# First FFT stage in bursts of eight tile matmuls, and the filters in four parts

## The chip, the cores and the metric

The kernel runs on one core of a Trainium2 chip. The metric is the time of one execution in microseconds; lower is better. The profile's span, from the first to the last instruction, is 1.7 to 1.9 us shorter than this time.

## The reference

A frequency filter over the sequence, then a dense layer with exact GELU and a second dense layer:

```python
X = np.fft.rfft(x, axis=1)                      # x: 8 images of 3008 x 256
y = np.fft.irfft(X * (filt_r + 1j * filt_i)[None], n=3008, axis=1)
h = y.reshape(24064, 256) @ w_in                # w_in: 256 x 2048
g = 0.5 * h * (1 + erf(h / sqrt(2)))
out = g @ w_out                                 # w_out: 2048 x 256, float32 out
```

## The kernel before

The transform of 3008 = 47 x 64 is done by matmuls in four stages with a reload through DRAM after the first and after the third. Image 0 is transformed in a head of its own. Images 1 to 7 are transformed under the dense layers: each step ("slot") of these emits four matmuls of the second layer (`mm2`, L493) and one product of the first (`mm1`, L466), and a table of slots says where the pieces of the transform go in between. In the traces TensorE's matmuls follow one another in the order in which they are emitted.

The first stage works with 47 x 48 tables, so the array is used as four tiles of 64 x 64 (the "tile mode"), each of which takes one matmul. The four start within 10 ns of one another in the trace; such a group is called a burst here:

```python
def s1(self, b, u):
    ...
    ps = [self.bank("ps_s1") for h in range(2)]          # two of three shared banks
    c, i = u // 2, 2 * (u % 2)
    for r in range(2):
        for h in range(2):
            w = 8 * c + 4 * r + i
            nc.tensor.matmul(ps[h][64 * r:64 * r + 64, :], lhsT=self.T1s[64 * h:64 * h + NA],
                             rhs=x[64 * h:64 * h + NA, w:w + 2, :], start=True, stop=True)
    for h in range(2):
        self._evac(a[:, h, i:i + 2, :].rearrange("p a b -> p (a b)"), ps[h], False)   # VectorE
    ...  # after every second burst: four stores of a to DRAM (R1)
```

The matmuls write to PSUM, in eight banks, and VectorE's copies out of it (`_evac`, "casts" in the views) make a bank free again. The banks belong to the first dense layer (three), the second (two) and the shared pool `f` (three). In the head they belong to other pools, `v` (five) and `t` (three):

```python
m.psum(wide, v=(5, 1), t=(3, 1))
for u in range(10):
    if u < 8:
        m.c3t(u)
    if u >= 2:
        m.c4(u - 2, (act, False if u > 7 else act))
wide.close()
m.psum(ctx, h=(3, 1), o=(2, 1), f=(3, 1))
```

The slots (`hi` is the first slot of the tokens of image b; `r1` and `r2` are the reloads, `s2` and `s4` the second and fourth stage):

```python
if b == 1:
    s1, n1, r1, s2, n2, r2, s4, n4 = 0, 1, 16, 26, 2.8, 61, 68, 0.72
else:
    s1, n1, r1, s2, n2, r2, s4, n4 = hi - 94, 1, hi - 78, hi - 71, 3.5, hi - 26, hi - 17, 1
```

## Time and profile before

| | before |
|---|---|
| median of the timed runs | 780.6 us |
| span of the profiled run | 780.6 us (this run took 782.4 us) |
| TensorE matmul busy | 98% |
| bursts of the first stage, images 1 to 7 | 56, of four matmuls |
| first weight load of the first dense layer | at 40.8 us |

TensorE is busy from 41 us to the end, so what counts is how long its stream is and where it waits. Three things are read in the prediction: what a burst adds to a slot, the wait ahead of the second stage (L300), and VectorE's filter products in the head.

### The profile page before, as it was taken

Reading aid. Unit: us, or ns where it says so; the run is one execution under the profiler, and the core shown is the slowest. Engines: PE = TensorE matmul, PEld = TensorE weight load, DVE = VectorE, ACT = ScalarE, POOL = GpSimd, SP = SyncE. Lnnn points to the kernel's source line nnn. Section 1 sums busy time; section 2 is a strip of 40 time slices with the busy share of each in tenths; the row PEclk is TensorE's granted clock in tenths of the full one; section 3 lists DMA queues with packets and bytes.
Section 4 is the critical chain, followed back from the end, with each engine's and each line's share of the span. In section 5 each row is a group of like instructions: output and inputs, shape, how many; then the busy total and the mean of one; then the engine's idle time right before and its main releaser. Section 6 shows DMA issues by size and latency. Waiting matters only on the chain.

```text
span 780.6 us, 14960 instructions
## 1 busy us (share of the span) xinstructions
PE 764.2 (98%) x5965; PEld 528.7 (68%) x6066; DVE 400.7 (51%) x722; ACT 568.4 (73%) x980; POOL 63.1 (8%) x157
## 2 busy tenths in 40 slices
PE   8999999999999999999999999999999999999998
PEld 5847665676766766577676767667776676766666
DVE  7866755473555635466354663546635465410011
ACT  6879855897558975589656896569865798666663
POOL 7801100020000100011000110001100000000000
PEclk9999999999999999999999999999999999999999
DMA  9794744465145651546515464255542522401111
GB/s 145 136 198 113 148 123 109 134 138 142 46 113 151 126 151 34 149 121 129 136 48 163 104 118 135 65 166 101 115 126 78 149 81 69 122 30 39 41 42 55
DMA packets 87270, 85.66 MB, mean 110 GB/s; under 512 B 6688, under 2 KB 77472, under 8 KB 87200
## 3 DMA queue, kind: packets, MB, share of 16 engines
q1 hardware_dynamic: 78816, 68.70, 31.0%
q0 software_dynamic: 8384, 16.00, 14.1%
q8 instruction: 47, 0.77, 0.4%
q14 instruction: 23, 0.19, 0.1%
HBM read 54.00 MB, written 46.66 MB: 129 GB/s over the span
## 4 chain that ended last, share of the span: by engine, by line
PE 86%; DMA 7%; POOL 2%; issue 1%; ACT 1%; DVE 1%; SPq 1%; POOLq 0%
PE ps_o L493 40%; PE ps_h L466 36%; PE ps_s L350 3%; DMA b_sb<-R 3%; PE ps_s L277 2%; PE ps_s L300 2%; PE ps_s L325 2%; DMA x_sb<-in_x_dram 2%; DMA R<-a_sb 1%; DMA F<-in_filt_i_dram 1%; POOL x_sb L82 1%; POOL F L96 1%; ACT g_sb L469 1%; SPq L286 1%; DVE a_sb L251 0%
## 5 line engine op out<-in xcount | busy, mean ns | idle before, releaser
L469 ACT ACTIVATE g_sb<-ps_h 128x512 bf16<-128x512 f32 x752 | 438.9, 597 | 189.4 <-PE ps_h L466 162.8
L493 PE MATMUL ps_o<-w_out_sb,g_sb 128*128 128x256 bf16 x2992 | 447.8, 273 | 3.6
L466 PE MATMUL ps_h<-y_sb,w_in_sb 128*128 128x512 bf16 (+3 forms) x1500 | 424.9, 365 | 0.4 <-DVE y_sb L253 0.4
L493 PEld LDWEIGHTS <-g_sb 128*128 128x128 bf16 x2992 | 282.1, 98 | 132.0 <-issue 10.9
L466 PEld LDWEIGHTS <-w_in_sb 128*128 128x128 bf16 x1600 | 154.5, 98 | 23.3 <-issue 1.6
L499 DVE COPY ost<-ps_o 128x512 f32<-128x512 f32 x93 | 63.8, 686 | 142.6 <-PE ps_o L493 141.1
L308 DVE TENSOR_TENSOR p<-ps_s,F 128x512 bf16<-128x512 f32 x84 | 58.0, 691 | 98.1 <-ACT p L307 85.1
L253 DVE TENSOR_SCALAR y_sb<-ps_s 128x376 bf16<-128x376 f32 x112 | 60.9, 548 | 80.8 <-PE ps_s L350 80.8
L251 DVE CAST a_sb<-ps_s 128x512 bf16<-128x512 f32 x112 | 72.1, 686 | 39.6 <-PE ps_s L277 38.4
L251 DVE CAST v_sb<-ps_s 128x512 bf16<-128x512 f32 x84 | 56.9, 684 | 4.5 <-PE ps_s L325 4.5
L306 ACT ACTIVATE p<-ps_s 64x512 bf16<-64x512 f32 x84 | 49.9, 594 | 2.9 <-PE ps_s L300 0.7
L307 ACT CAST p<-ps_s 64x512 bf16<-64x512 f32 x84 | 48.5, 577 | 1.0
L350 PEld LDWEIGHTS <-d_sb 96*128 96x128 bf16 x448 | 30.8, 97 | 25.6 <-DMA d_sb<-R 0.6
L101 POOL COPY gate<-p 1x1 bf16<-1x1 bf16 x48 | 8.5, 177 | 475.4 <-DVE p L310 475.4
L350 PE MATMUL ps_s<-T,d_sb 96*128 96x94 bf16 x448 | 36.3, 204 | 1.2
L310 DVE TENSOR_TENSOR p<-p 128x512 bf16<-128x512 bf16 x84 | 35.7, 425 | 2.9
L309 DVE TENSOR_TENSOR p<-p,F 128x512 bf16<-128x512 bf16 x84 | 34.8, 415 | 0.0
L300 PE MATMUL ps_s<-b_sb,T 128*128 128x256 bf16 x168 | 32.1, 272 | 1.9 <-DMA b_sb<-R 1.8
L82 POOL DMA_DIRECT2D x_sb<-in_x_dram x64 | 32.6, 511 | 13.3 <-issue 12.2
L325 PE MATMUL ps_s<-p,T 128*128 128x256 bf16 x168 | 32.1, 273 | 0.1
L325 PEld LDWEIGHTS <-T 128*128 128x128 bf16 x168 | 16.4, 98 | 20.1 <-DVE p L310 0.5
L300 PEld LDWEIGHTS <-T 128*128 128x128 bf16 x168 | 16.4, 98 | 16.2 <-issue 3.5
(103 smaller groups left out, 194.2 us busy)
## 6 DMA issues: line engine op xcount, KB each, us to landing
out_dram<-ost SPq DMA_DIRECT2D x93, 256.0 KB, 2.5
x_sb<-in_x_dram POOLq DMA_DIRECT2D x64, 188.0 KB, 3.9
R<-a_sb SPq DMA_DIRECT2D x112, 96.0 KB, 2.1
b_sb<-R SPq DMA_DIRECT2D x28, 384.0 KB, 4.5
R<-v_sb SPq DMA_DIRECT2D x42, 256.0 KB, 3.4
d_sb<-R SPq DMA_DIRECT2D x56, 192.0 KB, 4.8
w_in_sb<-in_moe_w_in_dram POOLq DMA_DIRECT2D x2, 512.0 KB, 10.4
w_out_sb<-in_moe_w_out_dram POOLq DMA_DIRECT2D x2, 512.0 KB, 11.1
```

What stands on the lines that cost most here:

```text
L251: self.nc.vector.tensor_copy(out=out, in_=in_)
L253: self.nc.vector.tensor_scalar(out=out, in0=in_, scalar1=scale, scalar2=None, op0=ALU.mult)
L300: nc.tensor.matmul(ps[:, 256 * i:256 * i + 256], lhsT=self.T2[:, k, 1:3].rearrange("p a b -> p (a b)"), rhs=self.st[b, "b", k // 6][:, k % ...
L306: nc.scalar.activation(out=p2[0:64], in_=ps[64:128], func=AF.Copy, scale=-1.0)
L307: nc.scalar.copy(out=p2[64:128], in_=ps[0:64])
L308: nc.vector.tensor_tensor(out=p1, in0=ps, in1=f(0), op=ALU.mult)
L325: nc.tensor.matmul(ps[:, 256 * i:256 * i + 256], lhsT=self.T3[:, k].rearrange("p a b -> p (a b)"), rhs=w[:, 256 * i:256 * i + 256], start= ...
L350: nc.tensor.matmul(ps[:, 94 * i:94 * i + 94], lhsT=d[:, (grp % 2) * 4 + i, 128 * half:128 * half + 128], rhs=t4, start=True, stop=True)
L466: nc.tensor.matmul(ps[:, o:o + n], lhsT=self.w_in_sb[:, dc, jc * 128:jc * 128 + 128], rhs=self.ring[:, dc, off:off + n], start=(dc == 0), ...
L469: nc.scalar.activation(out=self.st["g", t][:, jc, :], in_=ps, func=AF.Gelu)
L493: nc.tensor.matmul(ps[:, tile_i % 2, :], lhsT=g[:, jc, tile_i * 128:tile_i * 128 + 128], rhs=self.w_out_sb[:, jc, :], start=(jc == 0), sto ...
L499: nc.vector.tensor_copy(out=ost, in_=ps)
```

## The change

The intent: enter and leave the tile mode half as often, by doing two bursts in one. That takes four banks, one of which the dense layers lend. Around it the slots move, and in the head the filters come in smaller parts, with the copies arranged so that the filter products wait less.

```diff
-        ps = [self.bank("ps_s1") for h in range(2)]
-        c, i = u // 2, 2 * (u % 2)
... (signature, a's tile and the old loops left out)
+        ps = [[self.bank("ps_s1", "h" if i == h == 0 else "f") for h in range(2)] for i in range(2)]
+        for i in range(2):
+            for r in range(2):
+                for h in range(2):
+                    w = 8 * c + 4 * r + 2 * i
+                    nc.tensor.matmul(ps[i][h][64 * r:64 * r + 64, :], ...)
+        for i in range(2):
+            for h in range(2):
+                self._evac(a[:, h, 2 * i:2 * i + 2, :]..., ps[i][h], False)
... (stores as before, now after every burst)
-    for k, n in ((0, 4), (4, 8), (12, 12)):
+    for k, n in ((0, 4), (4, 4), (8, 8), (16, 8)):
         m.load_filters(k, n)
+    m.dup_filters(nc.gpsimd, 4, 4)
     m.load_w_in()
-    m.dup_filters(nc.gpsimd, 4, 8)
+    m.dup_filters(nc.gpsimd, 8, 8)
... (in the loop: dup_filters(16, 8) ahead of T1p, T1q and T1s in place of
     dup_filters(12, 4) ahead and dup_filters(16, 8) after; table_4 at q == 6, not q == 3)
-            s1, n1, r1, s2, n2, r2, s4, n4 = 0, 1, 16, 26, 2.8, 61, 68, 0.72
+            s1, n1, r1, s2, n2, r2, s4, n4 = 0, 4, 15, 25, 2.8, 61, 68, 0.72
-            s1, n1, r1, s2, n2, r2, s4, n4 = hi - 94, 1, hi - 78, hi - 71, 3.5, hi - 26, hi - 17, 1
+            s1, n1, r1, s2, n2, r2, s4, n4 = hi - 94, 3.5, hi - 80, hi - 69, 3.5, hi - 24, hi - 17, 1
```

More of the change, by code (lines that the diff above doesn't have):

```diff
@@ L262, in table_1_tiles, with s1 @@
             v.tensor_copy(out=self.T1s[r:r + NA, 0:48], in_=self.T1[0:NA, 0:48])
-    def s1(self, b, u):
+    def s1(self, b, c):
         nc = self.nc
-        if u % 2 == 0:
-            self.st[b, "a"] = self.pa.tile([128, 2, 4, 256], BF16, tag="a", name="a_sb")
-        if u == 0:
+        if c == 0:
             self.st[b, "R1"] = self.dram.tile([NB, 48, 256], BF16, tag="R1", name="R1")
-        a, R1, x = self.st[b, "a"], self.st[b, "R1"], self.st[b, "x"]
-        ps = [self.bank("ps_s1") for h in range(2)]
-        c, i = u // 2, 2 * (u % 2)
+        a = self.pa.tile([128, 2, 4, 256], BF16, tag="a", name="a_sb")
+        x = self.st[b, "x"]
+        ps = [[self.bank("ps_s1", "h" if i == h == 0 else "f") for h in range(2)] for i in range(2)]
[3 more added lines that the diff above has]
+                    w = 8 * c + 4 * r + 2 * i
+                    nc.tensor.matmul(ps[i][h][64 * r:64 * r + 64, :], lhsT=self.T1s[64 * h:64 * h + NA],
+                                     rhs=x[64 * h:64 * h + NA, w:w + 2, :], start=True, stop=True)
+        for i in range(2):
+            for h in range(2):
+                self._evac(a[:, h, 2 * i:2 * i + 2, :].rearrange("p a b -> p (a b)"), ps[i][h], False)
+        o = self.st[b, "R1"].rearrange("n q c -> q n c")
         for r in range(2):
             for h in range(2):
-                w = 8 * c + 4 * r + i
-                nc.tensor.matmul(ps[h][64 * r:64 * r + 64, :], lhsT=self.T1s[64 * h:64 * h + NA],
-                                 rhs=x[64 * h:64 * h + NA, w:w + 2, :], start=True, stop=True)
-        for h in range(2):
-            self._evac(a[:, h, i:i + 2, :].rearrange("p a b -> p (a b)"), ps[h], False)
-        if u % 2 == 1:
-            o = R1.rearrange("n q c -> q n c")
-            for r in range(2):
-                for h in range(2):
-                    w = HB * h + 8 * c + 4 * r
-                    nc.sync.dma_start(out=o[:, w:w + 4, :], in_=a[64 * r:64 * r + 48, h])
+                w = HB * h + 8 * c + 4 * r
+                nc.sync.dma_start(out=o[:, w:w + 4, :], in_=a[64 * r:64 * r + 48, h])
     def r1(self, b, c):
@@ L586 @@
             m.table_2_swap(1)
-            m.dup_filters(nc.gpsimd, 12, 4)
+            m.dup_filters(nc.gpsimd, 16, 8)
             m.T1p = g.tile([2 * NA, 2, K1, 2], BF16, name="T1p")
@@ L592 @@
             m.table_1_tiles(g)
-            m.dup_filters(nc.gpsimd, 16, 8)
             m.load_x(1)
@@ L603 @@
             else:
+                m.table_4()
                 m.c3(10, 1)
                 m.c3(11, 1)
-        if q == 3:
-            m.table_4()
         if q == 4:
@@ L633 @@
         if b == 1:
-            s1, n1, r1, s2, n2, r2, s4, n4 = 0, 1, 16, 26, 2.8, 61, 68, 0.72
+            s1, n1, r1, s2, n2, r2, s4, n4 = 0, 4, 15, 25, 2.8, 61, 68, 0.72
         else:
-            s1, n1, r1, s2, n2, r2, s4, n4 = hi - 94, 1, hi - 78, hi - 71, 3.5, hi - 26, hi - 17, 1
+            s1, n1, r1, s2, n2, r2, s4, n4 = hi - 94, 3.5, hi - 80, hi - 69, 3.5, hi - 24, hi - 17, 1
         for u in range(16):
-            if u % 2 == 0:
-                put(s1 + int(u * n1), m.s1, b, u // 2)
             put(s4 + int(u * n4), m.s4, b, u // 2, u % 2)
         for c in range(4):
+            put(s1 + int(c * n1), m.s1, b, c)
             put(r1, m.r1, b, c)
```

## The prediction

> **What bounds the kernel now.** I read the page first (busy shares, costliest groups), then the chain of work that ended last, the list of waits, and the timeline in three places: a stretch with first-stage bursts, the start of a second stage, and the head. The page:
>
> ```profile
> span 780.6 us, 14960 instructions
> PE 764.2 (98%) x5965; PEld 528.7 (68%) x6066; DVE 400.7 (51%) x722; ACT 568.4 (73%) x980; POOL 63.1 (8%) x157
> PEclk9999999999999999999999999999999999999999
> L493 PE MATMUL ps_o<-w_out_sb,g_sb 128*128 128x256 bf16 x2992 | 447.8, 273 | 3.6
> L251 DVE CAST a_sb<-ps_s 128x512 bf16<-128x512 f32 x112 | 72.1, 686 | 39.6 <-PE ps_s L277 38.4
> ```
>
> TensorE is the bound from about 41 us to the end: the chain is 86% PE, the clock is never withheld, VectorE is half idle. So time falls only where PE's stream gets shorter or where PE waits. The two dense layers fill that stream; the FFT stages of images 1 to 7 are spliced in between "slots" (one slot = four L493 and two L466 matmuls). A plain slot and one with a first-stage burst:
>
> ```profile
> 212.19 0.61 PE L493 MATMUL ps_o<-w_out_sb,g_sb 128*128 128x256 bf16 x4
> ...
> 213.07 0.60 PE L493 MATMUL ps_o<-w_out_sb,g_sb 128*128 128x256 bf16 x4
> ...
> 214.04 0.41 PE L277 MATMUL ps_s<-x_sb,T1s 47*64 47x512 bf16 x4
> ...
> 214.37 0.33 PEld L493 LDWEIGHTS <-g_sb 128*128 128x128 bf16 x4 [0.23 <-issue]
> 214.38 0.61 PE L493 MATMUL ps_o<-w_out_sb,g_sb 128*128 128x256 bf16 x4
> 214.49 0.69 DVE L251 CAST a_sb<-ps_s 128x512 bf16<-128x512 f32 x1 [0.91 <-PE ps_s L277]
> ```
>
> The reader is to see: slot to slot is 213.07 - 212.19 = 0.88 us, with a burst 214.38 - 213.07 = 1.31 us. A burst of four tile matmuls therefore costs 0.43 to 0.44 us. Its four matmuls start within 0.01 us (the trace's single records), so they run at once; streaming 512 columns takes 0.217 us (0.87 us per slot of 2048 columns, over four). The other 0.22 us is entering and leaving the tile mode: about 0.09 us before the first matmul and 0.12 us after the columns are through. There are 56 bursts, so 56 x 0.22 = 12.3 us of PE's time is switching.
>
> PE's other waits after the head are few: the start of the second stage, for the reload of the first stage's result.
>
> ```profile
> 330.22 0.59 PE L466 MATMUL ps_h<-y_sb,w_in_sb 128*128 128x512 bf16 x2
> 331.69 0.38 PE L300 MATMUL ps_s<-b_sb,T 128*128 128x256 bf16 x2 [0.87 <-DMA b_sb<-R]
> ```
>
> The last L466 matmul there starts at 330.44 and should hand over after 0.22; L300 starts 1.03 us late. The same start-to-start reading for images 2 to 6 gives 0.34, 0.40, 1.03, 0.40 and 0.41 us: 2.6 us. Image 1's later stages lose 0.14 and 0.23 us more. Nothing else over 0.06 us shows.
>
> The head, up to 41 us, hangs on VectorE's filter products:
>
> ```profile
> 16.38 2.36 DVE L393 TENSOR_TENSOR p<-ps_c,F 128x1024 bf16<-128x1024 f32 x2
> 19.43 2.35 DVE L393 TENSOR_TENSOR p<-ps_c,F 128x1024 bf16<-128x1024 f32 x2 [0.69 <-POOL F L96]
> 21.97 2.35 DVE L393 TENSOR_TENSOR p<-ps_c,F 128x1024 bf16<-128x1024 f32 x2 [0.20 <-issue]
> 24.79 2.35 DVE L393 TENSOR_TENSOR p<-ps_c,F 128x1024 bf16<-128x1024 f32 x2 [0.46 <-PE ps_c L388]
> 27.52 3.48 DVE L393 TENSOR_TENSOR p<-ps_c,F 128x1024 bf16<-128x1024 f32 x3 [0.37 <-POOL F L96]
> ```
>
> The filter copies on GpSimd hold it up twice, for 1.06 us together.
>
> **What the Trainium skill says.** "TensorEngine Tiling (Array Packing)", Key Properties: changing the tiling mode, not just the tile, drains TensorE. The trace agrees: 0.22 us per burst beyond the columns. "TensorE: Matmul & The Clock Gate", The mechanism (Part 3): a weight load overlaps a running matmul when its row group differs, or into the background weight buffer. The trace shows full-array weight loads lying under matmuls (PEld 68% busy under a PE that is 98% busy), but no burst of before loads the same tile twice, so for tiles it shows nothing. The Tiling page, PSUM Bottleneck: evacuation may become the limit after tiling. Here it nearly is for image 1 only (below).
>
> **The change, part by part.**
>
> Bursts. Eight bursts of four become four bursts of eight per image. The matmuls, casts and stores are the same in number. A burst of eight costs 0.09 + 2 x 0.217 + 0.12 = about 0.65 us against 2 x 0.435 = 0.87, saving 0.22 us. Images 2 to 7 have 24 such pairs: 24 x 0.22 = 5.3 us, all on PE's path.
>
> Banks. A burst takes all three shared banks and one of the three of the first dense layer. Four casts take 3 x 0.604 + 0.69 = 2.5 us (two in a row took 1.29) and begin 0.46 us after the burst does, so the banks are free 2.96 us after it. The next burst comes three or four slots later, 3 x 0.87 + 0.65 = 3.26 us at least; the output copies (0.69 us, slots 7 and 15 of sixteen) fall into the four-slot gap or after the last burst. The dense layer's lent bank is wanted two slots later and comes back after one cast. No stall for images 2 to 7.
>
> Image 1. Its slots have no L493, 0.44 us each, so bursts four slots apart come every 4 x 0.44 + 0.65 = 2.40 us. Four casts in a row take about 2.45 us, and ScalarE's four Gelus of 0.6 us take 2.4. VectorE already ran fourteen casts in 9.14 us there. I follow the banks: the burst's last bank is freed some 0.3 us late in most bursts. So of 4 x 0.22 = 0.9 us, 0.3 stays.
>
> Room for the reload. The last burst moves from 9 slots ahead of the second stage to 15. It took about 8.6 us from the last burst to the landing of the first reload (227.20 to 235.72); four casts at once instead of two add about 1.2 us. 15 slots give 13 us. So the 2.6 us of waits go. Image 1's shift (its third stage ends 9 slots, not 8, ahead of the fourth) takes most of the 0.23 us there: 0.2.
>
> Room lost. For images 2 to 7 the fourth stage now starts 10 slots after the last third-stage pair, not 12: 8.5 us instead of 10.3. From that pair's end to the landing of the first two reloads it was 8.5, 8.0, 7.6, 7.0, 7.7 and 8.1 us. That is tight; I allow 0.7 us over six images.
>
> Head. Same bytes, four more issues. The first copies need only filters 4 to 7 and should be done about 1 us sooner, which removes the 0.69 us wait of the second pair. But the third pair is then held by PE and ScalarE at nearly the old time (PE's L388 waited for ScalarE's copies just before), and w_in's issue now stands before copies 8 to 15. The last wait, 0.37, goes. Against it, the fourth table's two ScalarE copies (0.44 us together) move from a free place at 27.8 us to between the last third-stage copies, where the chain runs. I put the head at 0.2 us worse. Image 1's data are issued at about the old time and land 5 us ahead of use.
>
> Sum: -5.3 - 0.3 - 2.6 - 0.2 + 0.7 + 0.2 = -7.5 us: 780.7 - 7.5 = 773.2 us, 1.0%.
>
> **The rivals.** First, the second four matmuls may not overlap: a tile's weights could be loaded only once its running matmul has drained (a matmul record lasts 0.40 us). A burst then takes two full passes, about 0.86 us, and the burst term is nil or slightly negative. For it: the skill's stress on differing row groups. Against: the background buffer, and the full-array loads seen under matmuls. It leaves the reload term alone: about 778 us. I give it 15%. Second, casts become the bound: if VectorE falls behind, PE stands in the middle of a burst. For image 1 I count it; if it held for all, 0.3 us per burst would eat the gain and the time would be 777 to 779. VectorE's half-idle share speaks against. Third, the wait moves rather than goes: the second stage no longer waits for its reload, but the fourth does, up to 1 us per image; 776 to 777. Fourth, the head decides more than I think, either way by 1 us: 772 or 774.5.
>
> **Range and chances.** The main path gives 771.2 to 775; rivals one and three stretch it upward, so 771.2 to 777.2 holds it 8 times in 10. Two per cent is 15.6 us, more than all the switching (12.3 us) and waits (2.9 us) together, so faster by over 2% has 1%; slower by over 2% would need 0.6 us lost per burst on top, 1%; within 2%, 98%.
>
> **What would show it.** Bursts of eight whose second four start 0.22 us after the first, with 0.56 us from the first matmul to the next dense one, show the burst term right; second starts 0.4 us or more later show rival one. No idle ahead of L300, and at most 0.2 us ahead of each image's first L350, show the reload terms. In image 1's stretch, gaps inside bursts ended by VectorE are expected; elsewhere they would show rival two. The first L466 matmul, at 40.8 us now, gives the head: 41.0 expected. I am wrong if it is outside 40 to 42, or if PE's time between it and the end falls by less than 5 us.

## The result, and the profile after

The changed kernel took 774.41 us (median of 4 runs, 774.10 to 774.94), the kernel before 780.61 (4 runs, 780.45 to 780.78): ratio 0.9921, 95% interval 0.9904 to 0.9938. A ratio is the mean time of one kernel's fast runs over that of the other's of the same rounds, so it is not quite the ratio of the medians. Run again in a later batch (`e9_after_again`) it took 774.33 us against 782.17: ratio 0.9894.

The page of the changed kernel:

```profile
span 772.4 us, 14959 instructions
...
PE 757.2 (98%) x5965; PEld 528.4 (68%) x6066; DVE 397.8 (52%) x722; ACT 567.0 (73%) x980; POOL 64.8 (8%) x161
...
PE 96%; ACT 1%; DVE 1%; issue 1%; POOL 0%; DVEq 0%; POOLq 0%
```

PE was 86% of the chain that ended last and is now 96%; the 7% of DMA that the chain held before are gone. (Lines are numbered one lower than before: L276, L299, L349, L465 and L492 are what L277, L300, L350, L466 and L493 were.)

A burst of image 3 in the timeline (start, duration, engine, line, operation, count, and in brackets the engine's idle time):

```profile
212.95 0.60 PE L492 MATMUL ps_o<-w_out_sb,g_sb 128*128 128x256 bf16 x4
...
213.91 0.14 PEld L276 LDWEIGHTS <-T1s 47*64 47x64 bf16 x8
213.91 0.63 PE L276 MATMUL ps_s<-x_sb,T1s 47*64 47x512 bf16 x8
...
214.47 0.33 PEld L492 LDWEIGHTS <-g_sb 128*128 128x128 bf16 x4 [0.41 <-issue]
214.47 0.61 PE L492 MATMUL ps_o<-w_out_sb,g_sb 128*128 128x256 bf16 x4
```

All eight weight loads are through in 0.14 us, while the first four matmuls run. From the first burst matmul to the next dense one it is 214.47 - 213.91 = 0.56 us; the slot with its burst takes 214.47 - 212.95 = 1.52 us, against 0.87 to 0.88 for a plain one. So the burst costs 0.65 us. (Read from dense weight load to dense weight load it is 0.66, and 0.45 for a burst of four before.) The single records of this burst stand at 0, 3, 7, 10, 240, 243, 247 and 250 ns: the second four start 0.24 us after the first. All 24 bursts of images 2 to 7 look like this.

What the second stage waited for, from the view of its line, first before, then after:

```profile
L300 PE MATMUL ps_s<-b_sb,T x168: 269/273/273, 59.5 to 655.2; 128*128 128x256 bf16 x168
its engine sat idle before it (us, times) until:
  issue: 3.5, 6
  DMA b_sb<-R: 1.8, 5
```

```profile
L299 PE MATMUL ps_s<-b_sb,T x168: 272/273/273, 59.1 to 648.7; 128*128 128x256 bf16 x168
its engine sat idle before it (us, times) until:
who waited for it (us, times):
```

The list under "sat idle" is empty after. (Before, the two rows are PE's matmul and its weight load standing at the same places, so they are not added.) The fourth stage's list (L349) is empty too.

The head, in VectorE's filter products after the change:

```profile
16.40 4.82 DVE L392 TENSOR_TENSOR p<-ps_c,F 128x1024 bf16<-128x1024 f32 x4
22.03 2.51 DVE L392 TENSOR_TENSOR p<-ps_c,F 128x1024 bf16<-128x1024 f32 x2 [0.81 <-PE ps_c L387]
24.84 5.81 DVE L392 TENSOR_TENSOR p<-ps_c,F 128x1024 bf16<-128x1024 f32 x5 [0.30 <-POOL F L96]
```

The wait of 0.69 us on GpSimd ahead of the second pair has gone, but the third pair starts at 22.03, where it started at 21.97: the wait now ends with PE. And the end of the head, first before, then after, VectorE's last two copies and then PE:

```profile
39.50 1.17 DVE L253 TENSOR_SCALAR y_sb<-ps_c 128x376 bf16<-128x376 f32 x2
...
40.01 0.41 PE L277 MATMUL ps_s<-x_sb,T1s 47*64 47x512 bf16 x4
...
40.81 0.81 PE L466 MATMUL ps_h<-y_sb,w_in_sb 128*128 128x512 bf16 x2 [0.39 <-DVE y_sb L253]
```

```profile
39.79 1.17 DVE L253 TENSOR_SCALAR y_sb<-ps_c 128x376 bf16<-128x376 f32 x2
...
41.02 0.63 PE L276 MATMUL ps_s<-x_sb,T1s 47*64 47x512 bf16 x8 [0.64 <-DVE y_sb L253]
...
41.80 1.71 PE L465 MATMUL ps_h<-y_sb,w_in_sb 128*128 128x512 bf16 x7 [0.16 <-issue]
```

Before, image 1's first burst ran at 40.01 us, while VectorE still made the last two copies of image 0 (until 40.67); the first dense matmul waited for these, and the burst was free. After, the burst itself waits for them (until 40.96) and the dense layer starts behind it. (The first dense matmul's record is missing after: the weight loads show it at 41.57 us, and 40.78 before.)

**Where the time went.** I laid the two traces side by side by the weight loads of the first dense layer, 1600 in each, and took how much later (+) or sooner (-) the changed kernel is at the same load:

| at | changed kernel, us | step |
|---|---|---|
| first weight load | +0.79 | +0.79 |
| end of image 1's first stage | +0.46 | -0.33 |
| end of image 1's transform | +0.05 | -0.41 |
| end of image 2's | -1.21 | -1.26 |
| image 3 | -2.53 | -1.32 |
| image 4 | -4.48 | -1.95 |
| image 5 | -5.80 | -1.32 |
| image 6 | -7.14 | -1.33 |
| image 7, and to the end | -8.27 | -1.14 |

In each of images 2 to 7 the step has two parts, which the weight loads keep apart: over the stretch with the bursts it is 0.92 us (0.23 for each of four pairs), and at the start of the second stage it is the wait that has gone, in the order of the images 0.33, 0.39, 1.03, 0.40, 0.41 and 0.21 us.

### The profile page after: what moved, and what is told of

The parts are those of the page before. It is cut to its first block, busy times and chain, and to the rows that moved or that the text cites. A ratio compares the mean times of both kernels' runs of the same rounds, so it can differ in the third digit from the quotient of the medians.

```text
span 772.4 us, 14959 instructions
## 1 busy us (share of the span) xinstructions
PE 757.2 (98%) x5965; PEld 528.4 (68%) x6066; DVE 397.8 (52%) x722; ACT 567.0 (73%) x980; POOL 64.8 (8%) x161
## 4 chain that ended last, share of the span: by engine, by line
PE 96%; ACT 1%; DVE 1%; issue 1%; POOL 0%; DVEq 0%; POOLq 0%
PE ps_o L492 43%; PE ps_h L465 39%; PE ps_s L324 3%; PE ps_s L349 3%; PE ps_s L299 2%; PE ps_s L276 2%; PE ps_c L409 1%; PE ps_c L387 0%; PE ps_c3t L428 0%; ACT T L249 0%; PE ps_c L442 0%; ACT vt_sb L249 0%; PE ps_e L482 0%; PE ps_c1t L375 0%; ACT at_sb L249 0%
## 5 line engine op out<-in xcount | busy, mean ns | idle before, releaser
L492 PE MATMUL ps_o<-w_out_sb,g_sb 128*128 128x256 bf16 x2992 | 447.5, 273 | 2.1
L465 PE MATMUL ps_h<-y_sb,w_in_sb 128*128 128x512 bf16 (+3 forms) x1500 | 424.2, 365 | 0.2 <-issue 0.2
L492 PEld LDWEIGHTS <-g_sb 128*128 128x128 bf16 x2992 | 283.9, 98 | 134.4 <-issue 9.9
L465 PEld LDWEIGHTS <-w_in_sb 128*128 128x128 bf16 x1600 | 154.8, 98 | 23.2 <-issue 1.2
L251 DVE CAST a_sb<-ps_s 128x512 bf16<-128x512 f32 x112 | 69.5, 684 | 27.4 <-PE ps_s L276 27.1
L349 PEld LDWEIGHTS <-d_sb 96*128 96x128 bf16 x448 | 30.8, 97 | 25.2
L349 PE MATMUL ps_s<-T,d_sb 96*128 96x94 bf16 x448 | 36.3, 204 | 1.1
L299 PE MATMUL ps_s<-b_sb,T 128*128 128x256 bf16 x168 | 32.1, 273 | 0.0
L299 PEld LDWEIGHTS <-T 128*128 128x128 bf16 x168 | 16.4, 98 | 13.4
```

What stands on the lines that cost most here:

```text
L251: self.nc.vector.tensor_copy(out=out, in_=in_)
L299: nc.tensor.matmul(ps[:, 256 * i:256 * i + 256], lhsT=self.T2[:, k, 1:3].rearrange("p a b -> p (a b)"), rhs=self.st[b, "b", k // 6][:, k % ...
L349: nc.tensor.matmul(ps[:, 94 * i:94 * i + 94], lhsT=d[:, (grp % 2) * 4 + i, 128 * half:128 * half + 128], rhs=t4, start=True, stop=True)
L465: nc.tensor.matmul(ps[:, o:o + n], lhsT=self.w_in_sb[:, dc, jc * 128:jc * 128 + 128], rhs=self.ring[:, dc, off:off + n], start=(dc == 0), ...
L492: nc.tensor.matmul(ps[:, tile_i % 2, :], lhsT=g[:, jc, tile_i * 128:tile_i * 128 + 128], rhs=self.w_out_sb[:, jc, :], start=(jc == 0), sto ...
```

## The experiments

Twelve runs were made, in four batches on four chips, each batch with its own runs of the kernel before. Two things of the measuring come first, because they are larger than some of the effects.

The head is not the same in every run. Runs whose mean granted clock is below 1.000 took up to 4 us longer. This is what it looks like, in the windows view (stretch, its length, busy time of each engine, then the granted clock, DMA share and GB/s), first in the profiled run before, then in the profiled run of the experiment `e4_slots`, whose head has the same instructions:

```profile
10.00:15.00 5.00, 4.50 (x55) 2.97 (x55) 4.23 (x9) 3.54 (x8) 3.35 (x7) 1.00 1.15 187
```

```profile
10.00:15.00 5.00, 4.58 (x33) 2.80 (x31) 3.33 (x6) 2.49 (x6) 3.03 (x7) 0.50 1.11 182
```

At half the clock TensorE gets 33 matmuls done where it did 55, and the first dense weight load came at 43.43 us, not 40.78. So medians of a few runs mix two kinds. Below I give the medians and ratios, and beside them, from the profiled run, **the time from the first dense weight load to the end of the span**, which leaves the head out. For the kernel before it was 739.8, 739.2 and 739.6 us in three traces, for the changed kernel 730.8. The seven kernels with these bursts, it among them, lie between 730.0 and 731.2.

**The kernel before again (`e1_before_again`, `e12_before_third`).** No edit.

> The kernel before, unchanged, as a control. Its profiled run took 782.4 us where its timed runs took 780.6, so the first trace may show waits that most runs don't have. If the trace was a slow sample, the new span is near 778.9 us and the waits ahead of L300, 2.6 us in the first trace, are near 0.8 us. If the 2.6 us are real in every run, the new trace shows 2 us or more of them again. The ratio to before should be 1.000 within 0.001.

> The kernel before once more, for its trace on this chip. If this chip is one where before takes 780.6 us, the waits ahead of L300 should sum to less than 1 us and explain the smaller gain there (6.2 us against 8). If before takes 782 here, they sum to about 2.5 us again.

The first took 783.77 us (ratio 1.0007, interval 0.9982 to 1.0033), the second, a single run of unknown state, 783.45 us beside a median of 781.89. The waits ahead of the second stage were there again: 2.4 and 2.7 us over images 2 to 7 by the start-to-start reading (2.8 in the first trace), so they belong to ordinary runs of these chips. The wait ahead of image 1's fourth stage was not: 0.23 us in the first trace, 0.00 and 0.03 in these two. The run behind the first trace was 1.8 us slower than the median of the runs timed with it all the same. A chip on which the kernel before takes 780.6 us did not come up again: its medians in the four batches were 782.97, 782.17, 781.89 and 782.67.

**Bursts alone (`e2_bursts`).** The head of before, and the slots of the later stages as before:

```diff
+ s1 as in the changed kernel
+            s1, n1, r1, s2, n2, r2, s4, n4 = 0, 4, 16, 26, 2.8, 61, 68, 0.72
+            s1, n1, r1, s2, n2, r2, s4, n4 = hi - 94, 3.5, hi - 78, hi - 71, 3.5, hi - 26, hi - 17, 1
```

> Bursts of eight and their slots alone; the head and the second, third and fourth stages stand as before. My theory: 24 pairs x 0.22 = 5.3 us less for images 2 to 7, no wait ahead of L300 for these (13 slots of room, 11.3 us), image 1's first burst exposed (+0.65 us) since it needs a bank that is freed last, image 1 otherwise -0.5: about 774.3 us, as the whole change. Rival (the gain is the reload's waits and the slots, the bursts give less than 4 us): 777 or more.

775.28 us, ratio 0.9894 (0.9874 to 0.9913); its three runs at the full clock took 774.1 to 774.9, where before took 782.0 to 783.0. From the first dense weight load it is 730.9 us, 0.15 more than in the changed kernel, and this 0.15 us is a wait in image 1's third stage, which the changed kernel's shift of image 1 removes. No wait ahead of the second stage: the last of four bursts comes four slots sooner than the last of eight, and that alone makes room enough. The changed kernel's two extra slots for images 2 to 7 bought nothing further.

**The head alone (`e3_head`).** The changed kernel's head; bursts and slots of before.

> The head's part alone (filters in four parts, copies, fourth table later), bursts of four. My theory: the first L466 matmul 0.3 us later than before, 41.1 us, time +0.3 us: 780.9. Rival (the head's new order is what delays the first dense matmul by 1.0 us in the changed kernel): +1.0 us, first L466 at 41.8, 781.6.

782.74 us, ratio 0.9995 (0.9972 to 1.0019): not to be told from before. First dense weight load at 41.2 us; the rival's 41.8 did not come, so the head's new order is not what makes it late by 0.8 us.

**The slots alone (`e4_slots`).** Bursts of four as before:

```diff
-                hi - 94, 1, hi - 78, hi - 71, 3.5, hi - 26, hi - 17, 1
+                hi - 94, 1, hi - 78, hi - 69, 3.5, hi - 24, hi - 17, 1
```

> Only the second stage and the second reload two slots later for images 2 to 7; bursts of four as before. If waits ahead of L300 cost 2.6 us in an ordinary run and the later fourth-stage reload is free, 778.0 us. If an ordinary run has only about 0.8 us of them, 779.8. If the fourth stage then waits, up to 0.7 us of that comes back.

779.97 us, ratio 0.9957 (0.9936 to 0.9977). From the first dense weight load it is 737.1 us, 2.4 less than the mean of before (739.5), and PE's wait ahead of the second stage is gone. So the second stage's start is worth 2.4 us by two numbers in one line, without any change to the bursts. The fourth stage of images 2 to 7 did not wait. From here to the changed kernel's 730.8 it is 6.3 us, of which 5.5 us are in images 2 to 7, what the bursts give beyond the reload, and 0.8 us in image 1.

**The changed kernel again (`e9_after_again`).**

> The changed kernel unchanged, to have it beside the kernel before and the variants on one chip. From the bursts-alone run (774.3 us in its undisturbed runs on the chip where before took 782.4): 774.4, ratio 0.990.

774.33 us, ratio 0.9894 (0.9875 to 0.9913). One of six runs, the profiled one, took 2675.75 us, with every matmul slow (997 ns in the mean for one of the first dense layer, not 365) although its granted clock reads 1.000; it is left out, and I have no cause for it.

**Another lent bank for image 1 (`e5_o_bank`).** The second dense layer does not run yet when image 1's bursts do, so its banks lie idle:

```diff
-        ps = [[self.bank("ps_s1", "h" if i == h == 0 else "f") ...
+        ps = [[self.bank("ps_s1", ("o" if b == 1 else "h") if i == h == 0 else "f") ...
```

> Changed kernel, but image 1's bursts borrow a bank of the second dense layer, which does not run yet, in place of one of the first. My theory (the first burst stands 0.64 us because its lent bank is the one that VectorE empties last, and so no longer lies under the wait of the first L466): the first burst starts about 0.6 us sooner, the first L466 0.6 us sooner than in the changed kernel (41.2 us in a run whose clock is not withheld), time -0.6 us. Rival (the head is late for other reasons, such as the fourth table's copies): first L466 stays near 41.8, time unchanged.

775.77 us, ratio 0.9907 (0.9886 to 0.9928), four of six runs below the full clock; the two others took 774.4 and 774.5. My expectation failed: the first burst starts 0.06 us after VectorE's last copy ends, and the dense layer 0.61 us after it, exactly as in the changed kernel. I read the reason in the built program: the first matmul of the burst waits for the same counts of VectorE's and ScalarE's semaphores with either bank, those of the last copies out of the head's pool `v`. By this reading the wait comes with any bank that this pool held, not with the one that was emptied last; `e10_lent_last` and `e11_h_last` below test it.

**Old head (`e6_old_head`).** Bursts and slots of the changed kernel, head of before.

> Bursts and slots of the changed kernel with the head of the kernel before. My theory: the head part costs 0.3 us, so first L466 at 41.5 and time -0.3 us against the changed kernel. Rival: the head's new order pays, and this one is slower than the changed kernel.

774.01 us, ratio 0.9885 (0.9865 to 0.9905), all four runs at the full clock (773.7 to 774.1; the changed kernel's at the full clock in this batch: 774.0 to 774.4). That is 0.2 to 0.3 us, in the expected direction but within what I can tell apart. From the first dense weight load it is 730.8 us, the same.

**Five banks for image 1 (`e8_two_o`).** Head of before, and for image 1:

```diff
+        "o" if h == 0 else "f"        # b == 1
+        "h" if i == h == 0 else "f"   # b > 1, as in the changed kernel
```

> Head of before, bursts and slots of the changed kernel, and image 1's bursts on two banks of the second dense layer and two shared ones in turn, so that five banks serve a burst of four. My theory: the first burst starts near 40.1 us, the first L466 near 40.8 as in before, and the stalls inside image 1's second and fourth burst (0.39 and 0.36 us) fall below 0.1: -1.6 us against the changed kernel, the fastest of all. Rival (VectorE's casts bind image 1 whatever the banks): the stalls stay, -1.0 us or less.

773.14 us, ratio 0.9876 (0.9856 to 0.9896): the lowest ratio, though its interval overlaps with the changed kernel's. The stalls inside the second and fourth burst are gone. Image 1's second burst and its neighbours, in the changed kernel and then here:

```profile
43.44 1.04 PE L276 MATMUL ps_s<-x_sb,T1s 47*64 47x512 bf16 x8
44.41 1.90 PE L465 MATMUL ps_h<-y_sb,w_in_sb 128*128 128x512 bf16 x8
```

```profile
43.67 0.63 PE L276 MATMUL ps_s<-x_sb,T1s 47*64 47x512 bf16 x8
44.23 1.90 PE L465 MATMUL ps_h<-y_sb,w_in_sb 128*128 128x512 bf16 x8
```

0.97 us from burst to dense layer became 0.56. From the first dense weight load it is 730.0 us, 0.8 less, as the two stalls of 0.39 and 0.36 us say. The rival (VectorE binds whatever the banks) falls for these four bursts, but it was near: VectorE now makes twelve casts in 7.27 us without a gap, 2.4 us for four, as long as from one burst to the next (43.67 to 46.06). The other half of the expectation failed, as in `e5_o_bank`: the first burst still stood behind the last copy.

**Lent bank last (`e10_lent_last`).** As the last one, but image 1's first burst takes three shared banks first and the lent one for its sixth matmul:

```diff
-        "o" if h == 0 else "f"                                   # b == 1
+        "o" if (i == h == 1 if c == 0 else h == 0) else "f"      # b == 1
```

> As the last variant (head of before, image 1 on the second dense layer's banks), but image 1's first burst takes the lent bank for its sixth matmul, not its first. In the built program the wait for VectorE's and ScalarE's last copies of the head then stands at the sixth matmul. Theory: that wait belongs to any bank that the head's pool held, whichever it is, and five of the eight matmuls now run under it: first burst starts near 40.0 us in a run whose clock is not withheld, first L466 0.2 to 0.3 us sooner than with the lent bank first, time about -0.25 us against that variant. Rival (the burst waits for something else that VectorE does last): it starts at 40.5 or later, no change.

773.26 us, ratio 0.9890 (0.9878 to 0.9903). The burst now starts 0.66 us before VectorE's last copy ends, straight after the head's last matmul, as in the kernel before, and stands inside, at its sixth matmul:

```profile
41.45 1.12 PE L276 MATMUL ps_s<-x_sb,T1s 47*64 47x512 bf16 x8
42.73 1.49 PE L465 MATMUL ps_h<-y_sb,w_in_sb 128*128 128x512 bf16 x6 [0.16 <-issue]
```

The first dense weight load comes 0.39 us after that copy, not 0.61. So the wait goes with the place of the lent bank in the burst, and 0.22 us of the burst is hidden again. On the time this is too little to see: against `e8_two_o`, on another chip, the medians differ by 0.1 us the other way.

**Lent bank last in the changed kernel (`e11_h_last`).** Same edit, with a bank of the first dense layer:

```diff
-        "h" if i == h == 0 else "f"
+        "h" if i == h == (1 if b == 1 and c == 0 else 0) else "f"
```

> The changed kernel with one edit: the lent bank goes to the sixth matmul of image 1's first burst. Theory: first L466 at about 41.5 in place of 41.8 us, time -0.25 us. Rival: as in the changed kernel.

774.76 us, ratio 0.9919 (0.9904 to 0.9933); 774.3 to 774.9 at the full clock. A miss: the dense layer started 0.39 us after the copy, as hoped, but it then waited itself:

```profile
42.15 0.81 PE L465 MATMUL ps_h<-y_sb,w_in_sb 128*128 128x512 bf16 x3 [0.16 <-issue]
43.26 1.08 PE L465 MATMUL ps_h<-y_sb,w_in_sb 128*128 128x512 bf16 x4 [0.30 <-ACT g_sb L468]
44.54 0.63 PE L276 MATMUL ps_s<-x_sb,T1s 47*64 47x512 bf16 x8 [0.20 <-ACT g_sb L468]
```

Two of its own banks were still waiting for ScalarE's Gelu. From the first dense weight load it is 731.2 us, 0.4 more than in the changed kernel: more than the 0.22 us that was hidden in front is given back behind.

**Twice the switching (`e13_twos`).** The kernel before, with each burst of four of images 2 to 7 cut into two bursts of two with `mm2` between them:

```diff
... (s1 split in two; the second half put in after mm2)
-                put(s1 + int(u * n1), m.s1, b, u // 2)
+                put(s1 + int(u * n1), m.s1, b, u // 2, 0)        # two tiles, ahead of mm2
+                put(s1 + int(u * n1) + 0.5, m.s1, b, u // 2, 1)  # the other two, after mm2
```

> The suspected cost doubled: kernel before, with each burst of four of images 2 to 7 split into two bursts of two, a dense group of four L493 between them (image 1 has none there, so its halves stay together). My theory (a burst costs 0.22 us for entering and leaving the tile mode, plus 0.217 us for each pass of 512 columns, however many of the four tiles work): a burst of two costs 0.43 us, as one of four does, so 48 x 0.43 = 20.9 us more, about 803 us. Rival (a burst's time goes with the number of its matmuls, so that splitting adds only a little): under 10 us more.

805.14 us against 782.67, ratio 1.0287 (1.0268 to 1.0307): 22.5 us more. From the trace:

```profile
219.31 0.40 PE L279 MATMUL ps_s<-x_sb,T1s 47*64 47x512 bf16 x2
219.65 0.61 PE L497 MATMUL ps_o<-w_out_sb,g_sb 128*128 128x256 bf16 x4
220.19 0.40 PE L279 MATMUL ps_s<-x_sb,T1s 47*64 47x512 bf16 x2
220.53 0.61 PE L470 MATMUL ps_h<-y_sb,w_in_sb 128*128 128x384 bf16 x4
```

Two matmuls take 0.34 us to the next dense one, as four did (214.04 to 214.38 before), with the same 0.09 us on entering. So 48 x 0.43 = 20.9 us is what the added bursts cost; the waits ahead of the second stage also grew, from 2.4 to 2.8 us in three traces of the kernel before to 3.9 us here by the start-to-start reading. The rival falls: a burst's cost goes by entries and passes, not by matmuls. How much of the cost of an entry is draining the array, and how much anything else at the switch, no run here separates.

## Why the prediction was right

It said 773.2 us, and 774.41 was measured, within the range. Its own signs held too: the first L465 matmul is at 41.80 us (40 to 42 was asked for), and from the first dense weight load to the end the time fell by 9.1 us (at least 5). Term by term, the prediction's sum against the two traces laid side by side:

| term | predicted, us | traces, us |
|---|---|---|
| bursts of images 2 to 7 | -5.3 | -5.5 |
| bursts of image 1 | -0.3 | -0.3 |
| wait ahead of the second stage | -2.6 | -2.8 |
| image 1's later stages | -0.2 | -0.4 |
| fourth stage, images 2 to 7 | +0.7 | 0.0 |
| head | +0.2 | +0.8 |
| sum | -7.5 | -8.3 (before rounding) |

The head's miss (0.6 us too little) and the fourth stage's (0.7 too much) cancel; that the sum is so near is in part luck.

*Bursts.* Right, to about a hundredth: 0.65 us for a burst of eight was 0.65 to 0.66, and two bursts of four cost 0.02 more than the 0.87 it took. The first rival, a second four that must wait until the first has drained, is refuted by the second starts at 0.24 us. `e13_twos` shows the cost from the other side.

*Banks.* Right for images 2 to 7: no stall in 24 bursts, which refutes the second rival. For image 1 "some 0.3 us late in most bursts" was 0.39 and 0.36 us in two of four, and the fifth bank of `e8_two_o` takes both away, though VectorE then has no gap left.

*Room for the reload.* Right in kind, and shown apart from the bursts by `e4_slots`. The prediction put it to the move of the second stage together with the earlier end of the first; `e2_bursts` shows that the earlier end alone does it. Image 7's 0.21 us had been overlooked. (227.20 to 235.72 us is 8.5, not 8.6; nothing hangs on it.)

*Image 1's later stages.* Here the number was luck. The 0.2 us was to come from the wait ahead of image 1's fourth stage. That wait was 0.23 us in the trace that was read, but 0.00, 0.03, 0.05 and 0.00 us in `e1_before_again`, `e12_before_third`, `e3_head` and `e2_bursts`, which have this part of the slots as before, and 0.32 in `e4_slots`, so its absence after is not shown to come of the change. What the shift does remove is the other 0.15 us, in image 1's third stage: it stands in all these traces and in none with the shift.

*Room lost.* The 0.7 us for the fourth stage were not needed: the second of its reload pieces landed 0.3 to 1.2 us before the stage began, the first sooner. The third rival is refuted.

*Head.* The copies behaved much as described: the first wait on GpSimd went and came back as a wait for PE; another of 0.30 us remained, where none was expected. VectorE finished the head 0.29 us later than before, in one pair of traces. But the term missed what the lent bank does to image 1's first burst: it had been hidden under the wait for the last copy of image 0, and now it waits for that copy itself. This adds 0.49 us (0.61 us from the copy's end to the dense layer, not 0.12) in all five traces of kernels with the lent bank first. It is the prediction's largest omission; it was of the banks' ownership, which the listing of the head's pools would have told. That the new head order by itself costs or gains anything could not be shown: `e3_head` is at 0.9995, and in four traces at the full clock the head of the kernel before ended its last copy anywhere from 40.5 to 41.6 us.

*What stays open.* In the first result the gain was 6.2 us, in the batch of `e9_after_again` 7.8. The changed kernel took the same in both (774.4 and 774.3), the kernel before less in the first than later (780.6, not 782). Shorter reload waits in those runs would explain it, since only the kernel before has them, but none of them was traced, so this is argued, not shown. It also means that the sum, worked out on a trace of 782.4 us, was taken off a median of 780.6: had the two been told apart, the sum taken off that run would have given 774.9.

## What to carry to other kernels

Where small matmuls are packed into tiles between full-size ones, count the switches into and out of the tile mode: here each cost as much as streaming 512 columns, and putting two bursts together halved the number, in images 2 to 7 at no other cost, once there were banks for it. A buffer borrowed across a pool boundary brings that pool's last reader along as a wait, so look at what the first user of it was hidden under. And before crediting a schedule with removing a wait, move the schedule alone: the reload here was worth 2.4 us without any new burst.

## What the Trainium skill lacked or had wrong

- "TensorEngine Tiling (Array Packing)", Key Properties, says that a change of the tiling mode drains TensorE, and gives no cost there. Here a burst of 64 x 64 tiles among full-size matmuls took 0.22 us beyond its columns: 0.09 us on entering and 0.12 on leaving.
- "TensorE: Matmul & The Clock Gate", Part 3, says in one place that weights are pulled ahead for another row group or into the background buffer, and in its list "only when row_grp differs". Loads for the same four tiles ran ahead here: eight in 0.14 us, the second four matmuls 0.24 us after the first, where one matmul's record lasts 0.40 us (ends of such records are modelled). So the list is too narrow.
- The same page's packing model (one matmul and about 4 ns per further tile) has nothing to correct: four tile matmuls start within 10 ns, and with two tiles instead of four, for which it would have a burst 8 ns shorter (an estimate from that figure), the time to the next dense matmul was 0.336 us instead of 0.342.
- The same page, Part 1, has the clock at one half after an idle window of about 3.4 us. The half is what the trace of `e4_slots` shows (0.50 granted from 10 to 15 us), but no idle window of that length stands before it: TensorE's longest idle stretch after its first matmul was 1.79 us (7.59 to 9.38 us). What brought the half clock in some runs and not in others stays open.
